# Earlier loads for batch 2, weight sums ahead of the turning, and extra columns on VectorE, in a fused attention and gated feed-forward kernel

## The chip, the cores and the metric

The kernel runs on one core of one Trainium2 chip. The metric is the device time in microseconds (us) of one execution. A core has TensorE for matrix products (PE in the profile; PEld is its weight load, which runs beside the products), VectorE (DVE), ScalarE (ACT), GpSimd (POOL) and SyncE (SP). Matrix products land in PSUM, in banks of 128 x 512 float32. Each engine works through its own instructions in order. Loads and stores are issued from an engine's queue and carried out by 16 shared DMA engines.

## The reference

Eight batches, eight heads, 512 local and 32 global rows each, 64 columns a head. Local rows attend to the global rows and to their own neighbourhood of 32 rows on either side; global rows attend to everything. The result, 4352 rows of 512, goes through two weight matrices with a gelu-like gate between them.

```python
s_g = scale * q_g @ k_all^T                      # 32 global rows against all 544
out_g = softmax(s_g) @ v_all
s_ll = where(|i - j| <= 32, scale * q_l @ k_l^T, -1e9)
s_l = concat(scale * q_l @ k_g^T, s_ll)
out_l = softmax(s_l) @ concat(v_g, v_l)
x = concat(out_g, out_l) as (4352, 512)
h = x @ w_in                                     # 512 -> 2048
out = (h / (1 + exp(-1.702 * h))) @ w_out        # 2048 -> 512
```

## The kernel before

The order of every engine's work is written out by hand: instructions run on each engine in the order in which the code names them, and the framework adds only the waits that the data need.

**Attention.** The eight heads of a batch fall into two tiles of four (`Quad`, and `Wide` from batch 1 on), called `a` and `c` for u = 0 and 1. A tile's steps are methods: `Tk` and `Tq` turn keys and queries on VectorE in 32 x 32 blocks and copy the rows that are needed twice (`kcopy`, `qcopy`); `ext` writes the global rows into the turned tiles as extra columns, in four parts, on VectorE or, with `on_act`, on ScalarE; `S` makes scores on TensorE (L560), `X` exponentials on ScalarE (L571), `M` multiplies by the mask (L576); `U` and `Gm` are the products with the values (L586, L597), `R`, `XL` and `G` the normalization on VectorE. `XL` fills `xL`, the input of the feed-forward; `G` fills the same for the global rows.

**Feed-forward.** `h_mm` and `h_step` (L615) are the first product, 16 pieces `fc` of 128 columns with four matmuls each; `gelu` (L620) moves each piece out of PSUM on ScalarE. There are four PSUM banks for them, so the piece fc can start when the gelu of fc - 4 has emptied its bank; for fc 8 to 11 these are the gelus of fc 0 to 3, and for fc 12 it is that of fc 8, since fc 4 to 7 lie in the banks of the scores, emptied two at a time. The second product of batches 0 and 1 is `o_mm` (L655); from batch 2 on it is made with seven products instead of eight (`Pair`, L726), which need sums and differences of blocks of `w_out`. `weight_sums` makes these on VectorE, L671: 0, 3 and 4 have tiles of their own, 1 and 2 overwrite blocks of `w_out` and come later.

**Interleaving.** While batch i's first product runs, VectorE and ScalarE make the next batch's first tile ready. Around the change: the first product of batch 1 (L922 to L955), its gelus, and in between the turning and the extra columns of batch 2's first tile, the scores `a.S(0)` behind fc 13, and the weight sums at fc 3, 5 and 7 of that loop.

**Loads.** All float32 loads that become bfloat16 are issued from POOL's queue, one behind the other. `load(b, us)` loads queries and keys of a batch, both tiles or one; the row tiles `rk` and `rq` have two buffers each, so batch 2 uses batch 0's. `load_g(lo, hi)` loads global rows of keys and queries, `load_v` values. `load_rest` issues everything from batch 0's values to batch 1's. The loads of batches 2 and 3 are issued behind `behind(a.x...)` (L907), a copy of two elements on POOL that reads batch 1's `xL` and so holds the queue back until that is written.

Of the kernel before, what the change touches and what calls it, by code (L numbers as in the profile page):

```python
# [20 lines left out]
def kernel(  # L21
# [53 lines left out]
    def load(b, us=(0, 1), kq=True):  # L75
        if b not in loaded:
            loaded[b] = (ld.tile([128, 2, 16 * D], BF16, name="rk"),
                         ld.tile([128, 2, 16 * D], BF16, name="rq"))
        if kq:
            s = slice(us[0], us[-1] + 1)  # L80
            nc.gpsimd.dma_start(out=loaded[b][1][:, s], in_=qf[b][:, s])
            nc.gpsimd.dma_start(out=loaded[b][0][:, s], in_=kf[b][:, s])
# [5 lines left out]
    def v_view(b, n):  # L88
        return vtiles[b % 2][:, : 8 * n * (D + 2)].rearrange("p (u j c d) -> p u j c d", u=2, j=4, c=n)

    def load_v(b, hs=slice(0, 8)):
        if b == 2:
            nc.gpsimd.memset(v_view(b, 5)[:, :, :, :, D:], 1.0)
        vt = v_view(b, 5).rearrange("p u j c d -> p (u j) c d")
        vs, vg = (x[b].rearrange("h s d -> s h d") for x in (v_l, v_g))
        for c in range(5):
            n = 128 if c == 2 else 96
            nc.gpsimd.dma_start(out=vt[0:n, hs, c, :D], in_=vs[FIRST[c] : FIRST[c] + n, hs])  # L98
            if c != 2 and b != 1:
                nc.gpsimd.dma_start(out=vt[96:128, :, c, :D], in_=vg)  # L100

    def load_vg1():
        vt = v_view(1, 5).rearrange("p u j c d -> p (u j) c d")
        nc.gpsimd.dma_start(out=vt[96:128, :, 0, :D], in_=v_g[1].rearrange("h s d -> s h d"))
# [20 lines left out]
    def load_g(lo, hi, names="kq"):  # L125
        for name, dst, src in (("k", rkg, kgf), ("q", rqg, qgf)):
            if name in names:
                nc.gpsimd.dma_start(out=dst[:, lo:hi, :], in_=src[:, lo:hi, :])
# [93 lines left out]
    def make_mask(part):  # L222
        rnd, at, t0, t1, nr, base, rows = part
        src = band[:, base : base + 16 * nr].rearrange("p (r t) -> p t r", t=16)
        nc.gpsimd.tensor_copy(mask_at(rnd, at, t1 - t0, nr)[0:rows], src[0:rows, t0:t1])  # L225
# [14 lines left out]
    def transpose_g(lo, hi, names="qk"):  # L240
        for name, dst, s in (("q", qgT, rqg), ("k", kgT, rkg)):
            if name not in names:
                continue
            nc.vector.transpose(dst[:, lo:hi, :32], s[:, lo:hi].bitcast(F32))

    def load_v2(b):
        vp = v_l[b].rearrange("(u h) (c p) d -> u p h c d", u=2, p=128)
        for u in range(2):
            for p in (slice(0, 64), slice(64, 128)):
                nc.gpsimd.dma_start(out=v_view(b, 4)[p, u, :, :, :D], in_=vp[u, p])  # L250

    def load_rest():
        load_v2(0)
        n = d_ff // 4
        for part in range(4):
            if part == 3:
                for m in MASKS:
                    make_mask(m)
            for u in range(2):
                nc.gpsimd.dma_start(out=w_in_sb[:, part, 2 * u : 2 * u + 2],  # L260
                                    in_=w_in_r[u][:, :, part * n : part * n + n])
        for g4 in (1, 0, 2, 3):
            nc.gpsimd.dma_start(
                out=w_out_sb[:, 4 * g4 : 4 * g4 + 4, :].rearrange("p (g e) m -> p g (e m)", e=2),
                in_=w_out_r[:, 2 * g4 : 2 * g4 + 2, :])
            if g4 == 0:
                load(1, (0,))
                load_g(2, 4)
                load_vg1()
            if g4 == 2:  # L270
                load(1, (1,))
        load_v(1, slice(0, 4))
        load_v(1, slice(4, 8))

    xG = consts.tile([128, NKC, B * Sg], BF16)
    xG_by_row = xG.rearrange("p k (a s f) -> p k a s f", a=2, f=4)
# [7 lines left out]
    def spair():  # L284
        return [psS.tile([128, 2, 512], F32, name="s4", tag="s%d" % i) for i in range(2)]
# [333 lines left out]
    def gelu(out_, in_):  # L619
        nc.scalar.activation(out_, in_, AF.Gelu_apprx_sigmoid)  # L620
# [6 lines left out]
    def behind(x):  # L627
        nc.gpsimd.tensor_copy(spot_p, x)
# [7 lines left out]
    def h_act(i, fc, hp):  # L636
        n = width(i)
        gelu(gTs[i][:, fc, :n], hp[:, :n])

    def h_step(i, fc):  # L640
        if fc == 0:
            gTs[i] = (moe.tile([128, FC, TB], BF16, name="gT") if i < B else
                      early.bitcast(BF16).rearrange("p a b -> p (a b)").rearrange("p (f t) -> p f t", f=FC))
        hp = pbank("hp")
        h_mm(i, fc, hp, range(NKC))
        h_act(i, fc, hp)
# [20 lines left out]
    def weight_sums(*ks):  # L667
        for k in ks:
            x, y, op = ((b11, b22, ALU.add), (b12, b22, ALU.subtract), (b21, b11, ALU.subtract),
                        (b11, b12, ALU.add), (b21, b22, ALU.add))[k]  # L670
            nc.vector.tensor_tensor(wsum[k], x, y, op)  # L671
# [103 lines left out]
    a, c = Quad(0), Quad(1)  # L775
# [20 lines left out]
    cast_g32("k", rkg)  # L796
    transpose_g(0, 2, "k")
    load_rest()
    a.B(0)
    a.B(1, split=True)  # L800
# [62 lines left out]
    nq = {1: (Wide(2), Wide(3)), 2: (Wide(4), Wide(5))}  # L863
    a, c = nq[1]
# [40 lines left out]
    a.U(2)  # L905
    a.XL(1)
    behind(a.x[0:1, 1, 0:2])  # L907
    load(2, (0,))
    load_g(4, 8)
    load(2, (1,))  # L910
    load(3)
    load_v(2)
# [11 lines left out]
            h_mm(1, fc, hps[fc], kcs)  # L924
    a.G()
    c.G()
    nq[2][0].Tk()
    nq[2][0].Tq()
    transpose_g(4, 6)
    pt = spair()  # L930
    for fc in range(4, 8):
        h_mm(1, fc, bank(pt, (fc - 2) % 4), range(NKC))

    a, c = nq[2]
    for fc in range(FC):
        if fc in (3, 5, 7):
            weight_sums({3: 0, 5: 3, 7: 4}[fc])
        if fc == 11:
            c.Tk(False)
            c.Tq(False)  # L940
            c.ext((0, 1, 2))
            c.kcopy(nc.vector.tensor_copy)
            c.ext((3,))
            c.qcopy(nc.vector.tensor_copy)
        if fc < 4:
            h_act(1, fc, hps[fc])
        elif fc in (4, 6):
            f = slice(fc, fc + 2)
            gelu(gTs[1][:, f, :], pt[1 - (fc - 4) // 2])
        elif fc >= 8:  # L950
            h_step(1, fc)
        if fc in (4, 6, 8, 9):
            a.ext(((4, 6, 8, 9).index(fc),), on_act)
        if fc == 13:
            a.S(0)  # L955

# [245 lines left out]
```

## Time and profile before

| what | value |
|---|---|
| median of 3 runs | 287.18 us (286.78 to 289.01) |
| profiled execution | 288.3 us, span 286.5 us |
| TensorE busy | 278.6 us, 97% |
| VectorE busy | 204.7 us, 71% |
| ScalarE busy | 183.9 us, 64% |
| POOL busy | 95.1 us, 33% |
| granted TensorE clock | 0.998 |

The span runs from the first to the last instruction; the execution's time has 1.8 us more around it. The busy shares are means over stages. The part of the page that cuts the span into 40 equal slices of 7.2 us, each digit a busy share in tenths, shows TensorE at nine tenths or more in nearly all of them:

```profile
PE   7899999989999999999999999999999999999995
DVE  6680468678689899579957998679957697363352
ACT  3857657558678775688458783878468761864331
POOL 8974550765936100940068002910040000000001
```

In the ninth slice (57.3 to 64.5 us) it is at eight tenths. This is batch 1's first product, the stage that the change edits.

The traces name an instruction by its line, engine, operation and tile; a bracket behind it gives the idle time of the engine before it and what ended it.

### The profile page before, as it was taken

How to read it: one execution, taken by the hardware profiler on the slowest of the kernel's cores; microseconds unless marked ns; L12 is line 12 of the kernel's file. 1: busy time of each engine (PE TensorE's matmuls, PEld its weight loads, DVE VectorE, ACT ScalarE, POOL GpSimd, SP SyncE). 2: the span in 40 equal slices, each digit the busy share in tenths (PEclk: the TensorE clock that was granted, in tenths of full speed). 3: DMA queues.
4: the chain of work that ended last, by engine and by line, in shares of the span. 5: the costliest groups of instructions: out<-in, count | busy, mean ns of one | idle time of the engine just before them, and what ended most of it. 6: DMA issues, size and time to landing. Idle time of an engine off the chain costs nothing.

```text
span 286.5 us, 8846 instructions
## 1 busy us (share of the span) xinstructions
PE 278.6 (97%) x3727; PEld 179.0 (62%) x3727; DVE 204.7 (71%) x494; ACT 183.9 (64%) x297; POOL 95.1 (33%) x142
## 2 busy tenths in 40 slices
PE   7899999989999999999999999999999999999995
PEld 6554445434554478646884488647874589448884
DVE  6680468678689899579957998679957697363352
ACT  3857657558678775688458783878468761864331
POOL 8974550765936100940068002910040000000001
PEclk9999999999999999999999999999999999999999
DMA  7999995899999901794029903880122002200213
GB/s 203 174 194 210 203 141 83 148 212 134 152 168 194 152 3 39 82 188 83 2 77 153 159 6 76 79 87 5 28 51 73 2 3 76 73 0 2 73 35 115
DMA packets 59351, 28.23 MB, mean 99 GB/s; under 512 B 47472, under 2 KB 49776, under 8 KB 59312
## 3 DMA queue, kind: packets, MB, share of 16 engines
q0 software_dynamic: 51760, 17.83, 55.1%
q1 hardware_dynamic: 7120, 9.18, 11.6%
q10 hardware_dynamic: 432, 0.66, 0.7%
q8 instruction: 29, 0.48, 0.7%
q14 instruction: 10, 0.08, 0.1%
HBM read 36.31 MB, written 8.91 MB: 158 GB/s over the span
## 4 chain that ended last, share of the span: by engine, by line
PE 77%; DMA 10%; POOL 7%; issue 3%; DVE 1%; ACT 1%; POOLq 0%
PE hp L615 33%; PE px L726 13%; PE py L726 9%; PE x L726 6%; PE op L655 5%; PE s L560 5%; PE ov L586 5%; DMA rq<-in_q_l_dram 4%; DMA w_out_sb<-in_moe_w_out_dram 3%; DMA rk<-in_k_l_dram 2%; POOL w_in_sb L260 2%; POOL v L250 1%; POOL mask L225 1%; POOL v L98 1%; PE og L597 1%
## 5 line engine op out<-in xcount | busy, mean ns | idle before, releaser
L615 PE MATMUL hp<-xL,w_in_sb 128*128 128x512 bf16 x480 | 105.6, 379 | 1.5 <-ACT gT L620 1.3
L615 PEld LDWEIGHTS <-w_in_sb 128*128 128x128 bf16 x576 | 56.0, 98 | 61.6 <-issue 2.0
L620 ACT ACTIVATE gT<-hp 128x512 bf16<-128x512 f32 x120 | 69.7, 597 | 23.6 <-PE hp L615 22.0
L571 ACT ACTIVATE e<-s 128x1016 bf16<-128x1016 f32 (+1 forms) x56 | 53.2, 1003 | 25.3 <-PE s L560 25.3
L726 PEld LDWEIGHTS <-gs 128*128 128x128 bf16 x480 | 46.3, 98 | 6.4
L699 DVE TENSOR_TENSOR gs<-gT 128x512 bf16<-128x512 bf16 (+1 forms) x90 | 30.3, 363 | 17.5 <-ACT gT L620 17.3
L576 POOL TENSOR_TENSOR e<-e,mask 128x1760 bf16<-128x1760 bf16 x4 | 13.3, 3319 | 83.4 <-ACT e L571 83.4
L98 POOL DMA_DIRECT2D v<-in_v_l_dram x40 | 31.1, 780 | 14.9 <-PE og L597 4.3
L726 PE MATMUL py<-wsum,gs 128*128 128x256 bf16 x240 | 30.3, 273 | 0.0
L655 PE MATMUL op<-w_out_sb,gT 128*128 128x512 bf16 x128 | 29.5, 380 | 0.0
L576 DVE TENSOR_TENSOR e<-e,mask 128x1712 bf16<-128x1712 bf16 (+1 forms) x24 | 25.2, 1048 | 4.2 <-ACT e L571 4.1
L512 DVE STREAM_TRANSPOSE kT<-rk 128x512 f32<-128x512 f32 x14 | 14.6, 1045 | 17.4 <-DMA rk<-in_k_l_dram 17.4
L759 POOL DMA_DIRECT2D out_dram<-ob x2 | 1.2, 597 | 68.2 <-ACT ob L113 68.0
L655 PEld LDWEIGHTS <-gT 128*128 128x128 bf16 x128 | 11.8, 98 | 14.0
L726 PEld LDWEIGHTS <-gT 128*128 128x128 bf16 x192 | 18.0, 98 | 2.9
L726 PE MATMUL px<-w_out_sb,gT 128*128 128x256 bf16 x160 | 19.2, 273 | 0.0
L726 PE MATMUL px<-w_out_sb,gs 128*128 128x256 bf16 x160 | 19.1, 273 | 0.0
L471 DVE TENSOR_TENSOR xL<-ov,rs 128x512 bf16<-128x512 f32 x27 | 17.9, 686 | 0.7 <-PE ov L438 0.3
L696 DVE TENSOR_TENSOR gs<-gT 128x1024 bf16<-128x1024 bf16 (+1 forms) x30 | 17.3, 578 | 0.0
L560 PEld LDWEIGHTS <-kT 32*128 32x128 bf16 x672 | 12.5, 93 | 6.8 <-issue 5.7
L113 ACT ACTIVATE ob<-px 128x512 f32<-128x512 f32 x10 | 6.0, 598 | 15.2 <-DVE zz L748 15.2
L560 PE MATMUL s<-q,kT 32*128 32x160 bf16 (+1 forms) x448 | 14.7, 246 | 0.0
(154 smaller groups left out, 359.7 us busy)
## 6 DMA issues: line engine op xcount, KB each, us to landing
out_dram<-ob SPq DMA_DIRECT2D x128, 64.0 KB, 2.4
rq<-in_q_l_dram POOLq DMA_DIRECT2D x5, 512.0 KB, 8.0
rk<-in_k_l_dram POOLq DMA_DIRECT2D x5, 512.0 KB, 10.4
v<-in_v_l_dram POOLq DMA_DIRECT2D x24, 96.0 KB, 4.8
w_in_sb<-in_moe_w_in_dram POOLq DMA_DIRECT2D x8, 256.0 KB, 8.1
w_out_sb<-in_moe_w_out_dram POOLq DMA_DIRECT2D x4, 512.0 KB, 10.4
rk<-in_k_l_dram POOLq DMA_DIRECT2D x5, 256.0 KB, 7.9
rq<-in_q_l_dram POOLq DMA_DIRECT2D x5, 256.0 KB, 8.0
```

Source lines behind the costliest of these rows:

```text
L98: nc.gpsimd.dma_start(out=vt[0:n, hs, c, :D], in_=vs[FIRST[c] : FIRST[c] + n, hs])
L471: nc.vector.tensor_mul(self.x[:, 2 * self.u + h, :], self.st[1 + h], self.st["rs"])
L512: nc.vector.transpose(flat[:, 0:Sl].rearrange("p (r t) -> p t r", t=16), loaded[self.b][0][:, self.u].bitcast(F32))
L560: nc.tensor.matmul(bank(self.ps, j)[:, at : at + n], lhsT=self.k[p, KEYS[c] : KEYS[c] + 128, e], rhs=qs[p, :, :, e], start=(e == 0), stop= ...
L571: nc.scalar.activation(self.E[rnd][:, 2 * i : 2 * i + 2, :n], self.ps[i][:, :, :n], AF.Exp, scale=scale)
L576: eng.tensor_mul(e, e, mask[:, rnd : rnd + 1, :n].to_broadcast([128, 4, n]))
L615: nc.tensor.matmul(hp[:, : width(i)], lhsT=w_in_c[:, fc // 4, kc, fc % 4 // 2, :, fc % 2], rhs=(xL[i] if i < B else xG)[:, kc, :], start=( ...
L620: nc.scalar.activation(out_, in_, AF.Gelu_apprx_sigmoid)
L655: nc.tensor.matmul(op, lhsT=gTs[i][:, fc, tci * 128 : tci * 128 + 128], rhs=w_out_sb[:, fc, :], start=(first and fc == 4 * f4), stop=(fc = ...
L696: nc.vector.tensor_tensor(sums[i][2][:, g, :n], t[:, g, 0, :n], t[:, g, 1, :n], ALU.add)
L699: nc.vector.tensor_tensor(sums[i][k][:, g, : n // 2], x[:, g], y[:, g], op)
L726: nc.tensor.matmul(out_, lhsT=lv[:, g, tt * 128 : tt * 128 + 128], rhs=rv[:, g, :], start=(g == 0 and k in ((1, 3, 4, 6) if self.apart els ...
```

## The change

Three edits. The loads of the first half of batch 2's queries and keys (u = 0) and of the global rows of batches 2 and 3 go from behind L907 to the end of `load_rest`, behind batch 1's values. The three weight sums, so far issued at fc 3, 5 and 7 of batch 1's loop, go ahead of the turning of batch 2's first tile. And the extra columns of that tile, so far four copies on ScalarE between batch 1's gelus, are made on VectorE, right behind the turning of the global rows.

```diff
@@ load_rest
         load_v(1, slice(0, 4))
         load_v(1, slice(4, 8))
+        load(2, (0,))
+        load_g(4, 8)
@@ behind batch 1's attention
     a.XL(1)
     behind(a.x[0:1, 1, 0:2])
-    load(2, (0,))
-    load_g(4, 8)
     load(2, (1,))
     load(3)
     load_v(2)
@@ batch 1's first product
     a.G()
     c.G()
+    weight_sums(0, 3, 4)
     nq[2][0].Tk()
     nq[2][0].Tq()
     transpose_g(4, 6)
+    nq[2][0].ext()
     pt = spair()
     for fc in range(4, 8):
         h_mm(1, fc, bank(pt, (fc - 2) % 4), range(NKC))
 
     a, c = nq[2]
     for fc in range(FC):
-        if fc in (3, 5, 7):
-            weight_sums({3: 0, 5: 3, 7: 4}[fc])
         if fc == 11:
...
             gelu(gTs[1][:, f, :], pt[1 - (fc - 4) // 2])
         elif fc >= 8:
             h_step(1, fc)
-        if fc in (4, 6, 8, 9):
-            a.ext(((4, 6, 8, 9).index(fc),), on_act)
         if fc == 13:
             a.S(0)
```

## The prediction

> **What bounds the kernel now.** I read the list of waits first, for TensorE alone, from 63.4 us to the end. It has one entry:
>
> ```profile
> PE hp L615 <- ACT gT L620: 1.3, 1, 1.3
> ```
>
> From 63.36 us on TensorE waits for nothing else: the chain of waits runs over PE pieces alone from there to the last matmul at 282.9 us. So whatever ends before 63.4 us can only move the whole rest of the kernel, and the sum of the idle time there is the most that this change, which edits batch 1's first product and what lies around it, can win. The chain just ahead of that point (columns: start, us, what):
>
> ```profile
> 43.33 7.47 issue
> ...
> 51.87 6.92 DMA rk<-in_k_l_dram
> ...
> 58.81 1.06 DVE kT L512
> ...
> 61.39 0.31 ACT q L113
> 61.70 0.91 ACT gT L620
> ...
> 63.36 1.89 PE hp L615 x8
> ```
>
> A load issued at 51.87 lands at 58.79, VectorE turns it, ScalarE copies extra columns out of the turned rows, and only then comes a gelu that TensorE needs. The engines' timelines show why a copy for batch 2 stands ahead of batch 1's gelu (start, us; in brackets the idle time before and its releaser):
>
> ```profile
> 58.44 3.62 PE L615 MATMUL hp<-xL,w_in_sb 128*128 128x512 bf16 x16
> 63.36 1.89 PE L615 MATMUL hp<-xL,w_in_sb 128*128 128x512 bf16 x8 [1.31 <-ACT gT L620]
> 65.18 0.53 PE L560 MATMUL s<-q,kT 32*128 32x160 bf16 x16
> ```
> ```profile
> 56.91 1.02 ACT L620 ACTIVATE gT<-s 128x1024 bf16<-128x1024 f32 x1 [0.31 <-PE s L615]
> 61.39 0.31 ACT L113 ACTIVATE q<-qgT 128x128 bf16<-128x128 bf16 x1 [3.46 <-DVE qgT L244]
> 61.61 1.01 ACT L620 ACTIVATE gT<-s 128x1024 bf16<-128x1024 f32 x1
> ```
> ```profile
> 58.81 1.05 DVE L512 STREAM_TRANSPOSE kT<-rk 128x512 f32<-128x512 f32 x1 [3.58 <-DMA rk<-in_k_l_dram]
> 61.28 0.20 DVE L244 STREAM_TRANSPOSE kgT<-rkg 128x64 f32<-128x64 f32 x1
> 61.41 3.45 DVE L671 TENSOR_TENSOR wsum<-w_out_sb 128x2048 bf16<-128x2048 bf16 x3
> ```
> ```profile
> 41.25 2.08 POOL L98 DMA_DIRECT2D v<-in_v_l_dram x3 [1.99 <-DMA w_out_sb<-in_moe_w_out_dram]
> 50.81 0.18 POOL L628 COPY spot_p<-xL 1x2 bf16<-1x2 bf16 x1 [7.49 <-DVE xL L471]
> ```
>
> ScalarE works in order. Its first extra-column copy (61.39) waits 3.46 us for the turned global rows, and the gelu of fc 6 and 7, whose product TensorE had ready at about 58.6, stands behind it until 61.61. The gelu of fc 8 follows at 62.72, and TensorE's fc 12, which takes the PSUM bank that this gelu empties, starts 1.31 us late. VectorE meanwhile sits idle for 3.58 us, and POOL for 7.49.
>
> **The change, part by part.** Extra columns to VectorE. Four ScalarE copies go (0.31, 0.31, 0.26 and 0.42 us by their rows at 61.39, 62.51, 63.20 and 63.83), and with them the 3.46 us wait. The gelu of fc 6 and 7 then starts 0.3 us behind its matmuls, as its twin at 56.91 did: about 58.9 to 59.9. The gelu of fc 8 ends near 60.5 (0.60 each). Fc 12 can start when fc 11 is through, 58.44 + 3.62 = 62.06: a slack of about 1.6 us. The whole 1.31 us goes.
>
> What is late next? The scores of batch 2 (row 65.18, two fc steps of 0.9 us behind fc 12) would be due at 63.9. They need VectorE's whole chain, now with the sums ahead: the last instruction of batch 1's global rows ends at 55.23 (start 54.91, 0.32); three weight sums, 3.45 by their row, to 58.7; key and query turning with their copies and the two global transposes, 2.67 by the stretch from 58.81 to 61.48, to 61.35; four extra-column copies, 0.51 by the next tile's on VectorE (70.96 to 71.47), to about 61.9. That is 2.0 us before 63.9. On VectorE the four copies are new work of 0.51 us; their cover is idle time before batch 3's turning, which in the trace waits 1.02 us for its load. Without it they would cost nothing either: VectorE's next user on the path, the first mask product at 71.56, waits for an exponential that would end at 70.2.
>
> Weight sums. They fill VectorE's idle time, 55.23 to 58.81: 3.45 of 3.58 us, so turning starts at 58.7 instead of 58.81. What is queued behind them is just that turning; without the idle time they would cost the turning 3.45 us, of which 2.0 is slack. The first reader of a sum is the py matmul at 105 us. By themselves: nothing.
>
> The loads. Four issues (0.55, 0.55, 0.77 and 0.78 us on POOL) move from 51.33 to behind batch 1's last value load, which ends at 43.33. POOL is idle from there to 50.81, so they fit before the copy at 50.81 that held them back. On POOL's queue everything behind that copy moves up 2.55 us: batch 2's second half, batch 3's rows, batch 2's values. The buffer is batch 0's, whose half was turned within the first 10 us. POOL also seems to keep eight loads under way: behind eight issues from 51.33 on, the ninth comes at 58.83, just as the first pair lands. The first moved load would stand eight behind a value load issued at about 34.3, which even with the longest landing of a value load, 10.2 us, is through at 44.5; the last, eight behind the one at 37.36, goes by 47.6. Both lie before 50.81. The transfers go into quiet time (columns: stretch, busy us of PE, PEld, DVE, ACT, POOL; clock, DMA share, GB/s):
>
> ```profile
> 45.00:46.00 1.00, 1.00 (x24) 0.46 (x25) 0.65 (x2) 0.95 (x2) 0.00 (x0) 1.00 0.00 0
> ```
>
> They share the DMA engines with SP's output stores from 45.16 on; the first pair took 7.5 us beside stores (51.33 to 58.8), so about 51 to 52, at worst the 12.8 us of the longest load, about 57. VectorE asks at 58.7. Since the sums stand in front, the early landing itself is worth 0.1 us off the path. So I cost the loads at nothing. Not shown in the trace is what they do to the transfers ahead of them. The lower bound is a gain: the only other PE idle is 0.16 us at 53.26, so -0.16. The upper bound is a wait for batch 1's last values, priced below at 3.0 us. I take zero, the nearer row being the last three value loads, which landed within 2.9 us and left the DMA engines empty at 45.
>
> Sum: 286.5 - 1.31 = 285.2 us of span. The profiled execution took 288.3 with 1.8 around its span, so 287.0 on its scale. It lies 1.1 above the median of 287.18 (286.78 to 289.01), so on the median's scale 285.9.
>
> **A rule against it.** Weight sums and POOL's load issues met in the trace already: the issue at 62.19 took 0.89 us and that at 63.39 0.77, within sums that ran from 61.41 to 64.86; the same issue beside a transposition took 0.77 (68.49). That is 0.12 us at most. The Trainium skill, page "SBUF — State Buffer", in its warning on VectorE blocking DMA, says that VectorE's two-port operations lock GpSimd out for the whole instruction, so that it can't write descriptors for its loads. By that rule the three sums, now beside the issues from 51.33 on, could hold POOL back by up to 3.45 us; the rows here show a small part of it. By the rule the time is the first rival's, by the rows it is the sum above.
>
> **The rivals.** First, POOL held up: VectorE's sums stop the issues for their whole 3.45 us. Net of the 2.55 by which the queue moves up, batch 3's rows land 0.9 later than now, its turning and copies (3.24 us, from 68.23 to 71.47) end at 72.4, and the first mask product ends at 73.4 where it could have ended at 71.3. The second follows to 74.5 and batch 2's value product, due 75.74 - 1.31 = 74.4, waits some 0.1 to 0.3: about 286.1. Against it are the 0.89 and 0.77 above. The lock of which the Trainium skill's page speaks would do this.
>
> Second, the wait only changes its name: VectorE's chain ends 3.3 us later than worked out (2.0 slack + 1.31), the scores wait where fc 12 waited, and nothing is won: 287.2. For it: nine instructions in a row now have to keep their durations. Against: each has a row, and the rows were taken beside POOL issues.
>
> Third, slower: the moved loads delay the last value loads of batch 1 (issued from 41.25, the last at 42.67). They are read by the global and value products of the second tile at 49.83. It decides at a landing 49.83 - 42.67 = 7.2 us after issue for any wait, and 8.5 for a loss against before. With the longest landing of any value load, 10.2, TensorE waits 3.0 and the result is 287.18 - 1.31 + 3.0 = 288.9. At the longest of all loads, 12.8, it waits 5.6: 291.5. For it: in the busy stretches value loads did take so long. Against: the values are ahead in POOL's order, and landed in 2.8 and 2.9.
>
> Fourth, the loads don't start early, because something still holds the buffer. Then they land at 58.8 as now, the sums still fit in front of the turning, and the copies are still off ScalarE: 285.9 to 286.0, hardly another number. The gain hangs on ScalarE's queue, not on the loads.
>
> **How the numbers follow.** Chances: forecast, the fourth case included, 0.76; POOL held up 0.05; no gain 0.09; slower by late values 0.08; more than the stall, by scatter, 0.02. Predicted time 285.9. Range: down to 285.0, the forecast less half of the 1.8 us between the shown runs; up to 287.6, no gain and 0.4 of scatter (median to lowest). About 1% (2.9 us) is what a measurement can tell from no change. Faster by that would need twice the idle time that there is: 0.03. Slower by it needs a value landing of 11.4 us: 0.04. Within 1%: 0.93.
>
> **What would show it.** Right: on ScalarE the gelu of fc 6 and 7 at about 58.9, no L113 copies between the gelus; TensorE's fc 12 at 62.1 without idle time, the scores at 63.9; sums at 55.2 to 58.7; copies done by 62; loads issued 43.3 to 46. Wrong: a new entry in TensorE's list of waits, at 49.8 for values, at 63.9 for kT or q, or past 74 for a mask product; sums or copies much over 1.2 and 0.2 us each.

## The result, and the profile after

The changed kernel is slower: median 288.98 us (287.15 to 292.67, 22 runs) against 287.24 us (286.15 to 289.63, 22 runs) before, a ratio of 1.0061 with a 95% interval of 1.0041 to 1.0081. Its profiled execution has a span of 287.6 us, 1.1 more than before's. Line numbers between L274 and L907 stand two higher than before.

The wait that was to go is gone. ScalarE's timeline of the changed kernel (start, us; in brackets idle time and releaser) has no column copies between the gelus:

```profile
58.84 1.02 ACT L622 ACTIVATE gT<-s 128x1024 bf16<-128x1024 f32 x1 [0.31 <-PE s L617]
60.57 1.02 ACT L622 ACTIVATE gT<-s 128x1024 bf16<-128x1024 f32 x1 [0.70 <-PE s L617]
61.49 0.59 ACT L622 ACTIVATE gT<-hp 128x512 bf16<-128x512 f32 x1
```

VectorE's shows sums, turning and columns at their foretold lengths, 0.9 us later than foretold because the second tile's normalization ahead of them came late:

```profile
56.13 3.46 DVE L673 TENSOR_TENSOR wsum<-w_out_sb 128x2048 bf16<-128x2048 bf16 x3
59.52 1.03 DVE L514 STREAM_TRANSPOSE kT<-rk 128x512 f32<-128x512 f32 x1
...
62.25 0.22 DVE L547 COPY kT<-kgT 128x256 bf16<-128x256 bf16 x1
```

POOL's shows the moved loads where they were meant to be:

```profile
43.42 0.56 POOL L81 DMA_DIRECT2D rq<-in_q_l_dram  x1
...
45.23 0.79 POOL L128 DMA_DIRECT2D rqg<-in_q_g_dram  x1
50.91 0.17 POOL L630 COPY spot_p<-xL 1x2 bf16<-1x2 bf16 x1 [4.90 <-DVE xL L473]
```

What was lost stands in TensorE's timeline:

```profile
50.45 0.76 PE L588 MATMUL s<-e,v 128*32 128x128 bf16 x38
53.17 0.35 PE L588 MATMUL s<-e,v 128*32 128x72 bf16 x10 [1.95 <-issue]
...
60.37 5.34 PE L617 MATMUL hp<-xL,w_in_sb 128*128 128x512 bf16 x24
```

and in its list of waits from 28 us on, which has these two entries and no other:

```profile
PE s L588 <- issue: 2.0, 1, 2.0
PE ov L588 <- issue: 0.4, 1, 0.4
```

The 24 products from 60.37 on run without a gap: they are the pieces fc 8 to 13, inside which the kernel before stalled for 1.31 us. But TensorE stops for 1.95 us in the middle of the second tile's last value product, 38 products into a group of 48, and for 0.43 us at 83.3. "issue" means that the profile shows no semaphore and no operand that it waited for. The sum: -1.31, -0.16 (the small wait for xL, now hidden), +1.95, +0.43 and 0.10 from the start make +1.0, and the spans differ by 1.1.

What can stop TensorE without a wait? Its instructions are themselves brought by DMA. The page's third part lists a queue "instruction" (q8) with 29 packets and 0.48 MB. Its packets are 16,384 bytes each in the trace, and 29 of them for TensorE's 7454 products and weight loads make 257 instructions a packet, so the queue is taken for TensorE's. The view of the DMA queues for the stretch from 46 to 50.5 us (packets, MB, share of 16 engines' time; packets that overlap count twice; q1 has the output stores) reads, before:

```profile
q1 hardware_dynamic: 340, 0.47, 41.2%
q8 instruction: 1, 0.02, 1.5%
q14 instruction: 1, 0.01, 0.6%
```

and after:

```profile
q0 software_dynamic: 1276, 0.56, 106.2%
q1 hardware_dynamic: 237, 0.34, 21.9%
q14 instruction: 1, 0.01, 0.4%
```

The moved loads (q0) fill a stretch that held output stores and instructions alone, and the packet of q8 is no longer in it. It came at 47.66 before and at 50.83 after; TensorE went on 1.37 us after it was through at 51.80.

The Trainium skill, page "Runtime: NRT & Kernel Launch", section on instruction fetch mechanics, says that an engine's instructions are refilled in 16 KiB blocks of 256 by the sequencer's own DMA queue, at a cost that it calls "mostly hidden". The packets here have that size; before, the cost was hidden, after, it was not.

### The profile page after: what moved, and what is told of

Its sections match the earlier page's. It is cut to its first block, busy times and chain, and to the rows that moved or that the text cites. A ratio compares the mean times of both kernels' runs of the same rounds, so it can differ in the third digit from the quotient of the medians.

```text
span 287.6 us, 8846 instructions
## 1 busy us (share of the span) xinstructions
PE 278.2 (97%) x3727; PEld 178.8 (62%) x3727; DVE 205.1 (71%) x498; ACT 183.6 (64%) x293; POOL 95.2 (33%) x142
## 4 chain that ended last, share of the span: by engine, by line
PE 93%; DMA 2%; POOL 1%; issue 1%; ACT 1%; DVE 0%; POOLq 0%
PE hp L617 39%; PE px L728 13%; PE op L657 10%; PE py L728 9%; PE x L728 6%; PE s L562 6%; PE ov L588 5%; PE s L617 2%; DMA rq<-in_q_l_dram 2%; PE s L588 1%; PE og L599 1%; PE ov L440 1%; ACT e L387 0%; PE s L359 0%; PE ov L425 0%
## 5 line engine op out<-in xcount | busy, mean ns | idle before, releaser
L100 POOL DMA_DIRECT2D v<-in_v_g_dram x24 | 14.1, 588 | 4.7 <-DMA rq<-in_q_l_dram 4.7
```

## The experiments

Theory: the moved loads hold back the packet with TensorE's next 256 instructions; TensorE runs out of them where its instructions are shortest. Rivals: the sums or the copies cause the stall, or the value product waits for data of its own.

### Each part alone

**Loads back** (e1): the change, but with the loads where they were.

```diff
         load_v(1, slice(4, 8))
-        load(2, (0,))
-        load_g(4, 8)
...
     behind(a.x[0:1, 1, 0:2])
+    load(2, (0,))
+    load_g(4, 8)
```

> The change without its moved loads: weight sums ahead, extra columns on VectorE. Theory (the moved loads' packets hold back TensorE's next block of instructions): no idle time of TensorE inside the second tile's value products at 51 us, none at 63 us either; 1.3 us under the kernel before, about 285.9. Rival (sums ahead or the copies on VectorE make the 51 us stall or a later one): a stall of 2 us stays, and the time is that of the changed kernel, about 289.

Measured: 286.71 us (286.34 to 288.37, 12 runs), ratio to before 0.9988 (0.9973 to 1.0003): the loss is gone, but the median is 0.5 us under before and not 1.3. The trace has no stall in a value product; it lacks the records of 23 products, and the 0.3 us of "issue" in two op groups are such holes:

```profile
PE op L655 <- issue: 0.3, 2, 0.2
PE hp L615 <- DVE xL L471: 0.2, 1, 0.2
```

**Loads alone** (e2): before, with the loads moved and nothing else.

> Only the loads moved; sums and extra columns as before. Theory: the turning starts right behind batch 1's global rows (about 55 to 56), so ScalarE's copies no longer hold the gelu and the 1.31 us go; but the stall inside the second tile's value products at 51 us is there, 1.5 to 3 us; time 288 to 289.5. Rival (the stall needs the sums or the copies): no stall at 51, 285.9.

Measured: 288.66 us (287.15 to 291.66, 12 runs), ratio 1.0051 (1.0019 to 1.0083). The trace (with the same kind of holes) has both stalls:

```profile
PE s L588 <- issue: 1.9, 1, 1.9
PE ov L588 <- issue: 0.5, 1, 0.5
```

The turning started at 55.67 and no gelu held TensorE back. The moved loads alone make the loss; a part of the sums or copies in it does not show.

**Columns alone** (e3): before, with the extra columns on VectorE behind `transpose_g(4, 6)`.

> Only the extra columns on VectorE; loads and sums as before. Theory: the whole gain of the change, since the wait was ScalarE's queue: TensorE's fc 12 starts without idle time, no stall at 51; 285.9. Rival (the sums must stand ahead, or the scores at 64 wait for the copies): 0 to 0.6 us of gain only.

Measured: 286.92 us (286.57 to 287.30, 12 runs), ratio 0.999 (0.9977 to 1.0002). The trace has neither stall and its span is 285.1, so the wait was ScalarE's queue, as said. But the median gained 0.3 us, not 1.3, and the interval reaches 1.

**Sums alone** (e4): before, with `weight_sums(0, 3, 4)` behind `c.G()`.

> Only the weight sums ahead of the turning. Theory: nothing; the turning starts at 58.8 as before, ScalarE's copy waits until 61.4, TensorE stalls 1.3 us at 62; 287.2. Rival (the sums beside POOL's issues hold the loads back): turning and copies later, 0.5 us or more above before.

Measured: 287.72 us (287.25 to 288.56, 10 runs), ratio 1.0022 (1.0009 to 1.0036): a small loss where I had expected none. The rival named 0.5 us, but for a later turning, and the turning starts earlier than before (58.39 against 58.81). The trace explains the loss together with e3:

```profile
PE hp L615 <- ACT gT L620: 0.8, 1, 0.8
```
```profile
55.01 3.46 DVE L671 TENSOR_TENSOR wsum<-w_out_sb 128x2048 bf16<-128x2048 bf16 x3
58.39 1.03 DVE L512 STREAM_TRANSPOSE kT<-rk 128x512 f32<-128x512 f32 x1
```

The turning waits for no load here; it waits for the sums. With the copies still on ScalarE that sets a floor under the stall, 0.8 us, whenever the load lands; e4's median lies 0.80 us above e3's, which has no such stall. Before, the stall depends on when the load lands: in the trace of e3 the turning can start at 58.05, in that of before at 58.81. The executions of before that ran beside these (35) begin at 286.45, e3's at 286.57, e4's at 287.25: the best of before can have had next to no stall.

**Before once more** (e6), unchanged, for a second profile.

> The kernel before, unchanged, for another profile. The runs with columns alone gave 0.3 us, not 1.3, though their traces have no idle time at 63. If the profiled execution of before was one with a long wait, another shows the load of batch 2's keys landing earlier than 58.8, at 58.0 to 58.4, and an idle time of 0 to 0.9 us ahead of fc 12, span about 285.5. If not, 1.3 us again, span 286.5, and the missing 1 us is lost elsewhere.

Measured: the turning at 58.84 again and a wait of 1.9 us, time 288.34. So this expectation failed as it was put. But both profiled executions of before, 288.3 and 288.34, lie high: of the 35 executions of before beside e1 to e4 only 4 took 288.3 or more. What the typical execution loses at fc 12 is better taken from e3: about 0.3 us. There is no trace of an execution of before near the median.

### The place of the stall

**After once more** (e7), unchanged.

> The changed kernel, unchanged, for another profile. Theory: the stall at 51 is there again, 1.5 to 4 us, at the same place in the count of instructions, ending about 1.4 us after the packet with the next instructions. Rival (an accident of one execution): no stall, span 284.9.

Measured: 289.65 us; TensorE waits 2.7 and 0.5 us on "issue", at the same two products. In both traces 733 products of the program come ahead of the one and 1115 ahead of the other; these counts are their numbers below. In the trace of e7 the records show the packet from 51.10 to 52.08 and TensorE going on at 53.34, 1.3 us behind its end.

**Code shifted** (e5): the changed kernel with 32 more products of zeros near its start.

```diff
-    fill(8, a.bk[1][3])
+    fill(40, a.bk[1][3])
```

> The changed kernel with 32 more warm-up products of zeros near its start (40 for 8), which add 64 instructions to TensorE ahead of everything and nothing else. Theory (a block of 256 instructions comes late): the stall at 51 keeps its place in the count of instructions, so it moves 32 products ahead in the program: from 10 before the end of the second tile's last value product (L588, the group with 72 elements) to its first value product or the one of ones, 22 to 30 products earlier, near index 733 counted with the added ones. Rival (that product waits for something of its own, values or VectorE): it stays at the same product, index 765. Time: 0 to 2 us above the changed kernel, since the added products may delay the start.

Measured: 289.73 us. The stall at 51 did not move, it went away: TensorE is 2.0 us later at that place than in the changed kernel's first trace, while the loads still start at 43.2, and the packet, at 49.44 to 50.78, is in time. Up to 19 us the delay is 0.8 us. The rest comes with a stall at number 350:

```profile
20.40 1.24 PE L617 MATMUL s<-xL,w_in_sb 128*128 128x512 bf16 x5 [1.06 <-issue]
```

The packet ahead of it came from 18.07 to 19.02, and TensorE went on 1.4 us after its end. The moved loads, issued from 43.2 us on, have no part in it: with 32 products more ahead, TensorE comes to number 350 at 19.3 us instead of 21.2, ahead of the packet's instructions. The stall at 83 us answers the question of the place. In the changed kernel it stands behind 48 of the 72 products of its group:

```profile
82.37 0.55 PE L588 MATMUL ov<-e,ones 128*32 128x128 bf16 x24
82.74 0.54 PE L588 MATMUL ov<-e,v 128*32 128x128 bf16 x24
83.72 0.55 PE L588 MATMUL ov<-e,v 128*32 128x128 bf16 x24 [0.43 <-issue]
```

and with the code shifted behind 16:

```profile
82.51 0.41 PE L588 MATMUL ov<-e,ones 128*32 128x128 bf16 x16
83.46 0.32 PE L588 MATMUL ov<-e,ones 128*32 128x192 bf16 x8 [0.54 <-issue]
83.60 0.91 PE L588 MATMUL ov<-e,v 128*32 128x128 bf16 x48
```

48 products are through before the stall in the first fence (24 and 24), 16 in the second: 32 fewer, as many as were added ahead. In the count it is number 1115 again. The places agree to the instruction: from number 350 to 733 there are 383 products with their weight loads and two semaphore instructions of TensorE, 768 in all, which is three times 256. A stall that keeps its place in the count of instructions and changes the product waits for the instructions.

### The transfer ahead of it

**Loads held** (e8, and e11 for its interval): the changed kernel with the loads behind a copy that reads the second tile's last mask product.

```diff
     c.M(1)
+    behind(c.E[1][0:1, 0, 32:34])
+    load(2, (0,))
+    load_g(4, 8)
```

> The changed kernel with its moved loads held behind a copy that reads the second tile's last mask product, so that they are issued from about 49.6 us instead of 43.4, still ahead of the copy that waits for xL. Theory: the block of instructions that is fetched at 47.6 is through before them, so no stall at 51; about 286.7, as with the loads back. Rival (any load ahead of the copy stalls the value products): a stall of 1 us or more at 51, 288 or more.

> The version with the loads held, once more, for its interval: 0.2% under before (0.5 us), 286.6, its executions within 1 us of each other where before's spread over 3 and the changed kernel's over 5.

Measured: 286.60 us (286.20 to 287.13, 10 runs), ratio 0.998 (0.9962 to 0.9999), and again 286.59 us (286.03 to 288.03, 12 runs), 0.9983 (0.9963 to 1.0003). From 28 us on the two traces have the 0.2 us wait for xL and nothing else. The same loads, 6 us later and still ahead of their old place, do no harm, since the packet, at 47.67 and 47.47, is through before them. Its median is the lowest of all versions, 0.1 us under e1's, which the scatter does not tell apart; that it beats before rests on intervals that end at 0.9999 and 1.0003. Its executions spread over 0.9 and 2.0 us, so the expected 1 us held once.

**Global rows only** (e9) and **queries and keys only** (e10) early.

> The changed kernel with only the global rows (128 KB of the 640) loaded early; the first half of batch 2's queries and keys is back behind the copy that waits for xL. Theory (the fetch is served when the loads ahead of it have drained): they are issued at 43.4 and 44.2 and land by about 49; the packet with the next block starts at 47.6 to 49 and TensorE waits 0 to 0.3 us at 51. Rival (any early load does it, whatever its size): 1.5 us or more.

> The changed kernel with only queries and keys (512 KB) loaded early; the global rows are back behind the copy. Theory: the two land at 49.5 to 50, so the packet starts at 49 to 50 instead of 50.8 to 51.1, and TensorE, which goes on some 1.4 us behind the packet's end, waits 0.5 to 1.5 us at 51 instead of 2.0 to 2.7. Rival (the fetch does not go with the loads' landing): 0, or 2 us and more.

Measured, e9: no stall, 288.36 us. This execution lost its time elsewhere: TensorE idled from 6.29 to 8.21 us and was granted half its clock from 9 to 12 us, so that it is 1.5 us late at 52; the packet at 49.22 is in time for that. The two loads had landed by 47.6 us, before the packet starts in the kernel before (47.66). e10: 287.81 us, with

```profile
PE s L587 <- issue: 1.0, 1, 1.0
PE ov L587 <- issue: 0.3, 1, 0.3
```

The size counts: no stall, 1.0, and 1.9 to 2.7 us for 128, 512 and 640 KB with the code unshifted, from one to three traces for each size; the 1.0 us and the packet at 49.10 are as e10 expected.

**More early** (e12): the changed kernel with `load_g(4, NQ)` for `load_g(4, 8)`, and without the later `load_g(8, NQ)`.

> The changed kernel with all remaining global rows of queries and keys (batches 2 to 7, 384 KB instead of 128) loaded early, and not in batch 1's second product. Theory (the fetch waits for the loads ahead): the loads land at about 52 to 53 instead of 51.3, the packet starts 1 to 2 us later than 50.8 to 51.1, and TensorE waits 3 to 4.5 us at 51; median 1 us or more above the changed kernel's 289, and more executions with a mean granted clock of 0.994. Rival (the fetch has a fixed delay once anything is in the queues): 2 to 2.7 us, 289.

Measured: 291.22 us (289.48 to 292.68, 4 runs), ratio 1.0132 (1.0079 to 1.0184). The time came out as foretold, the mechanism only in part. The packet was not later than in the changed kernel (50.70), and the stall at 51 was 2.7 us, as the rival had it. The additional time is a stall at a third place, number 987. That is 128 products with their weight loads, 256 instructions, ahead of number 1115, and 254 of both with four semaphore instructions, 512, behind number 733:

```profile
PE s L588 <- issue: 2.7, 1, 2.7
PE og L599 <- issue: 2.0, 1, 2.0
```

and a lower clock behind the first stall (columns: stretch, its length, busy us of PE, PEld, DVE, ACT, POOL with counts; granted clock, DMA share, GB/s):

```profile
52.00:53.00 1.00, 0.00 (x0) 0.00 (x0) 0.00 (x0) 0.00 (x0) 1.00 (x4) 1.00 1.19 197
53.00:54.00 1.00, 0.82 (x12) 0.41 (x12) 0.43 (x1) 0.00 (x0) 1.00 (x3) 0.84 1.23 216
54.00:55.00 1.00, 1.00 (x4) 0.34 (x3) 0.96 (x4) 0.00 (x0) 1.00 (x2) 0.50 1.02 203
```

Taken together (from the records of the instruction packets and products in the traces; the fourth column counts the weight loads that TensorE has begun when the packet starts):

```
kernel             early loads   packet        begun  stall at 51
before             none          47.66-48.77   601    none
before again (e6)  none          47.09-48.16   602    none
loads back (e1)    none          47.60-49.12   602    none
columns alone (e3) none          48.15-49.40   604    none
sums alone (e4)    none          47.51-49.20   601    none
loads held (e8)    from 49.4     47.67-49.05   603    none
held again (e11)   from 49.6     47.47-49.30   601    none
global rows (e9)   128 KB        49.22-50.98   602    none
queries, keys e10  512 KB        49.10-50.17   643    1.0
code shifted (e5)  640 KB        49.44-50.78   632    none
loads alone (e2)   640 KB        50.20-51.26   711    1.9
after              640 KB        50.83-51.80   725    2.0
after again (e7)   640 KB        51.10-52.08   734    2.7
more early (e12)   896 KB        50.70-51.78   734    2.7
```

So it is the packet that is late and not TensorE that is early: undisturbed, it starts at 601 to 604 of TensorE's weight loads, some 130 ahead of number 733, and in the changed kernel at 725, while TensorE still runs. In the five stalls TensorE goes on 1.3 to 1.5 us after the packet's end. How long the packet waits does not follow the bytes beyond 640 KB, nor the landing of the last load; on which DMA engine it waits, and behind what there, these traces do not say. That stays open.

The stall at 83 us has a packet of its own, at 78.52 to 79.52 before and 81.38 to 82.25 after. The moved loads had landed at 51.3. What differs ahead of that packet is batch 4's rows, 1 MB, which POOL's queue, moved up, issues 3 us earlier; before and after (the first of two issues):

```profile
77.84 0.73 POOL L81 DMA_DIRECT2D rq<-in_q_l_dram  x1
```
```profile
74.76 0.74 POOL L81 DMA_DIRECT2D rq<-in_q_l_dram  x1
```

In the five traces with a stall at number 1115 this issue starts from 73.66 to 74.96, in the eight without one from 75.63 to 77.84. In e12 it starts at 71.67, and the packet ahead of number 987 comes at 78.82 (71.99 before). That fits the same mechanism, but no run moves these rows alone.

## Why the prediction was wrong, point by point

- **ScalarE's queue as the bound at 63 us: right.** e3 removes it alone, and so does e2, where the turning comes early enough.
- **Its size, 1.31 us: mis-sized.** It was read from an execution at the upper end of before's. Columns alone gained 0.3 us in the median. The prediction noted that the profiled execution lay 1.1 above the median, and took the gain over to the median's scale whole; the stall itself is most of that 1.1.
- **Weight sums at nothing: right with the copies off ScalarE, wrong alone.** In the changed kernel the scores followed fc 13 without a gap. Alone the sums cost 0.5 us (e4).
- **"So I cost the loads at nothing": the step that failed.** The bounds named what the loads could do to other transfers, and then priced only the value loads. These landed within 3.3 us of their issue in the changed kernel. The transfer that suffered is in no list of the kernel's loads, since no line issues it: TensorE's instructions, in the page's third part as q8. Its price was 1.95 + 0.43 us in the profiled execution, 2.7 + 0.5 in another. By the issue times above the 0.43 goes with the queue's moving up, which the prediction had worked out (2.55 us) and used in its first rival alone.
- **The rivals.** The third had the sign, the place (TensorE, at 50 us, by the moved loads) and nearly the time (288.9; 288.98 was measured), with the wrong victim. That the time met is luck: its wait of 3.0 us is the longest landing of a value load, and its gain of 1.31 us is the one that e3 put at 0.3. The first fell: the sums ran from 56.13 to 59.59, and the two issues at 56.65 beside them took 1.67 us together, against 1.65 for the two at 72.56 in the kernel before, beside which VectorE was idle for all but the first 0.1 us. So the lock of which the Trainium skill's page "SBUF — State Buffer" warns did not show; whether these sums are two-port operations no run here shows. The second fell, since the scores did not wait. The fourth fell, since the loads started at 43.42; that the gain does not hang on them was right.
- **The early landing, "worth 0.1 us off the path": right,** and it is why the move could only lose: VectorE asked for the rows at 59.5, and they had been there since about 50.
- **The chances.** Within 1% was the case; the range, which ended at 287.6, did not allow for a cost outside the lists.

## What to carry to other kernels

A stretch in which the DMA engines look idle may be what lets the next block of instructions through in time. Where an engine runs many short instructions (here the 128 products ahead of number 733, with their weight loads, in 2.3 us), look for the instruction queue's packets before moving loads there, and move them behind the packet, or not at all if the rows are not asked for. And read a stall's size from several executions, or from an edit that removes it, before it is taken over to the median.

## What the runs showed of the hardware

TensorE's instructions arrive in transfers that compete with the kernel's own: a packet of 16,384 bytes, due at about 47.7 us, came 3 us late behind 640 KB of loads, and TensorE stopped at the packet's boundary. The stalls lie 768, 512 and 256 instructions apart.

A stall can cost more than its length. In e12 the granted clock fell to 0.50 for 3.41 us behind an idle time of 2.74 us, in e9 behind one of 1.92 us; after 2.70 us in e7 it did not fall. The traces' clock records fit one rule: the clock changes only on a grid of 3.41 us (in e12 the stretches are 14, 1 and 69 times that long), whose start differs from execution to execution. The 2.74 and the 1.92 us lay within one step of the grid. The 2.70 us were split by it into 1.79 and 0.91, the 1.95 us of the changed kernel's first trace into 0.80 and 1.15, the 2.0 us at number 987 in e12 into 1.78 and 0.22, and after none of these the clock fell. So far as these traces go, 1.92 us of idle time in one step halves the next, and 1.79 does not.

Seven of the 22 executions of the changed kernel had a mean clock of 0.993 or 0.994 and took 290.08 to 292.67 us, the other 15 took 287.15 to 289.62. With the loads alone it was 4 of 12, with more early 3 of 4; with the loads back or the columns alone it was none of 24, with the sums alone none of 10, in before beside them 2 of 35, with the loads held 1 of 22. That the seven lost their clock at the 51 us stall is likely by this but not shown: of the executions with that stall and a lower mean clock only e12's profiled one has a trace, and it lost the clock there. The Trainium skill, page "TensorE: Matmul & The Clock Gate", part 1, gives half rate after an idle window of about 3.4 us; here a window idle for 1.92 us was enough.
